# Earlier loads for batches 2 and 3, and x of batch 2 transposed entirely by DMA, in a one-core attention and MLP kernel

## Chip, cores, metric

One core of a Trainium2 chip. The metric is the device time of one execution in microseconds (us), the median over the executions named. Kernels are compared only within the same rounds.

## The reference, cut to what matters

```python
# q, k, v: (8 batches, 8 heads, 576 tokens, 64)
scores = q @ k.T / 8 + alibi_bias            # causal window of 128 tokens
x      = softmax(scores) @ v                 # -> (4608 tokens, 512)
h      = x @ w_in                            # 512 -> 2048   "first layer"
out    = (h * cos(h)) @ w_out                # 2048 -> 512   "second layer"
```

## The kernel before

The 4608 tokens are cut into nine chunks of 512. While chunk c goes through the layers, the attention of batch c + 1 is worked on in the gaps. The kernel has no fixed order of instructions: a list scheduler in the kernel's own Python (`Plan`) draws the order of every engine at build time from modelled durations. On the chip each engine follows that order and waits on semaphores where data is late.

A unit of attention (a head pair and 256 tokens, or the 64-token tail of a batch) ends with x in token-major form (`xnat`). The first layer needs it transposed (`xT`), in one of two ways: by a DMA that SyncE issues, or on TensorE into PSUM, from which ScalarE or VectorE copies it:

```python
def x_back(b, u, s, i):
    ...
    if b > 2 or (b == 2 and G):           # G: first (0) or second (1) 256 tokens of the batch
        o = op("sp", [lambda e: e.dma_start_transpose(xT[...], xnat[i][:, :])], ...)
        xops.append(o)
        return
    def f(e):                             # two 128x128 transposes on TensorE ...
        for r in range(2):
            ins = e.transpose(dst[:, 128*r:128*r+128], xnat[i][:, 128*r:128*r+128], ident[:, :])
        return ins
    op("pe", f, ...)
    flex(xT[:, pr, t0:t0 + 256], dst, ...)   # ... and a copy out of PSUM (ScalarE or VectorE)
```

The loads are issued by GpSimd, in program order, and cast from float32 to bf16. From the main loop:

```python
for c in range(NCH):
    ...                                   # first layer of chunk c
    if c + 1 < B:
        us = units(c + 1)
        if c == 0:
            play(1, SECOND)               # batch 1: its q and k are transposed on TensorE
        else:
            cross_transposes(c + 1)       # q, k of batch c + 1 by DMA
            if c == 1:
                load_v(2, after=crossed[3:4])   # waits for the fourth of these transposes
                load_qk(3)
                load_v(3)
            for g in range(0, 9, 3):
                run(us[g:g + 3], (1, 2, 3))
    if c == 0:
        load_qk(2)
    ...                                   # second layer of chunk c
R.schedule()
```

The softmax here doesn't subtract the row's maximum and nothing guards it: scores larger than these inputs give would overflow.

## Time and profile before

| | before |
|---|---|
| time, median of 3 | 313.05 us (312.87 to 313.22) |
| span of the profiled execution | 311.4 us |
| TensorE busy | 302.1 us, 97% |
| transposes of x on TensorE / by DMA (without tails) | 40 / 44 |
| GpSimd's wait ahead of V of batch 2 | 23.1 us |

To read the lines: a row of a timeline is start, duration, engine, line of the kernel, operation, output <- inputs, shapes, count, and in brackets the idle time before it with what ended it. A matmul's duration includes its way through the pipeline, so neighbours overlap; for the cost of one, take the distance from its start to the next start. In a list of waits a row is: who waited <- for whom: us in total, times, longest. The prediction below shows the page's main lines and reads them.

### The profile page before, as it was taken

What the parts mean: (1) busy time and instruction counts of PE and PEld (TensorE: products, weight loads), DVE (VectorE), ACT (ScalarE), POOL (GpSimd) and SP (SyncE); (2) the same over time, 40 slices, a digit from 0 to 9 for tenths busy, and PEclk for the clock granted to TensorE, in tenths of its full rate; (3) what the DMA queues carried; (4) which work ended last, traced back from release to release, by engine and by line L of the source; (5) the groups of instructions that cost most, each with busy time, mean ns of one, the idle gap of its engine ahead of it and who ended that gap; (6) DMA issues with size and microseconds to landing.
All of it is one profiled execution on the core that took longest, in us unless ns stands there. A gap on an engine that the chain in (4) does not pass through costs nothing.

```text
span 311.4 us, 6714 instructions
## 1 busy us (share of the span) xinstructions
PE 302.1 (97%) x2647; PEld 178.0 (57%) x2684; DVE 196.8 (63%) x444; ACT 206.7 (66%) x303; POOL 105.8 (34%) x134
## 2 busy tenths in 40 slices
PE   8799999999999999999999999999999999999996
PEld 4578546785578557845854554455445544444444
DVE  3798675786568757875887458766866882353000
ACT  7798936787588759773986488848873884462211
POOL 8999820069506300870537055505000000000000
DMA  9999999999939992999999999999823200101112
GB/s 131 166 193 193 192 171 193 164 105 167 189 76 121 154 171 47 120 152 191 141 175 158 176 138 108 147 169 138 144 59 103 70 8 2 68 0 67 69 67 101
DMA packets 159742, 38.97 MB, mean 125 GB/s; under 512 B 147808, under 2 KB 155232, under 8 KB 159712
## 3 DMA queue, kind: packets, MB, share of 16 engines
q0 software_dynamic: 109552, 18.10, 80.0%
q1 hardware_dynamic: 50160, 20.46, 33.5%
q8 instruction: 21, 0.34, 0.5%
q14 instruction: 9, 0.07, 0.1%
HBM read 36.70 MB, written 9.44 MB: 148 GB/s over the span
## 4 chain that ended last, share of the span: by engine, by line
PE 86%; DMA 8%; POOL 3%; issue 1%; DVE 1%; ACT 0%; POOLq 0%
PE ps L863 37%; PE ps L837 20%; PE ps L852 18%; DMA qnat<-in_q_dram 6%; PE ps L631 4%; PE ps L725 3%; DMA knat<-in_k_dram 2%; PE ps L728 2%; POOL vp L463 1%; PE ps L800 1%; PE ps L711 1%; PE ps L546 1%; PE ps L713 1%; PE ps L621 1%; POOL qnat L427 0%
## 5 line engine op out<-in xcount | busy, mean ns | idle before, releaser
L863 PE MATMUL ps<-w_outb,gT 128*128 128x512 bf16 (+2 forms) x564 | 133.7, 373 | 2.2 <-issue 0.8
L829 DVE TENSOR_TENSOR gT<-ps,cos 128x512 bf16<-128x512 f32 x144 | 94.8, 686 | 27.7 <-PE ps L863 14.0
L823 ACT ACTIVATE cos<-ps,halfpi 128x512 f32<-128x512 f32 x144 | 94.9, 687 | 20.9 <-PE ps L837 6.7
L863 PEld LDWEIGHTS ps<-w_outb,gT 128*128 128x128 bf16 x592 | 52.6, 98 | 53.1 <-issue 1.4
L668 ACT ACTIVATE p<-ps 128x768 bf16<-128x768 f32 (+1 forms) x64 | 54.8, 919 | 27.5 <-PE ps L631 15.3
L852 PE MATMUL ps<-xT,w_inb 128*128 128x256 bf16 x576 | 67.5, 273 | 0.0
L837 PE MATMUL ps<-xT,w_inb 128*128 128x512 bf16 x280 | 63.9, 379 | 0.6
L463 POOL DMA_DIRECT2D vp<-in_v_dram x40 | 34.8, 909 | 79.8 <-DMA xT<-xnat 35.2
L852 PEld LDWEIGHTS ps<-xT,w_inb 128*128 128x128 bf16 x576 | 54.5, 98 | 7.2 <-issue 0.5
L837 PEld LDWEIGHTS ps<-xT,w_inb 128*128 128x128 bf16 x288 | 27.3, 98 | 32.2 <-DVE xtail L756 1.1
L419 ACT ACTIVATE ob<-ps 128x512 f32<-128x512 f32 (+2 forms) x24 | 14.0, 582 | 44.2 <-PE ps L863 44.2
L454 POOL DMA_DIRECT2D qnat<-in_q_dram x32 | 29.3, 915 | 26.1 <-DMA xT<-xtail 26.1
L686 DVE TENSOR_TENSOR p<-p,emask 128x1024 bf16<-128x1024 bf16 x32 | 22.0, 688 | 13.7 <-ACT p L668 13.5
L454 POOL DMA_DIRECT2D knat<-in_k_dram x32 | 29.3, 917 | 2.1 <-PE ps L713 2.1
L767 DVE TENSOR_TENSOR xnat<-ps,rec 128x256 bf16<-128x256 f32 x64 | 26.8, 421 | 2.0
L725 PEld LDWEIGHTS ps<-vp,p 128*128 128x128 bf16 x256 | 17.0, 97 | 15.0 <-issue 8.8
L725 PE MATMUL ps<-vp,p 128*128 128x65 bf16 x256 | 21.9, 193 | 0.5 <-DVE p L686 0.4
L691 DVE TENSOR_TENSOR p<-p,emask 128x256 bf16<-128x256 bf16 x32 | 9.1, 283 | 17.6 <-ACT p L668 17.1
L728 PE MATMUL ps<-vp,p 128*128 128x65 bf16 x192 | 20.0, 193 | 0.0
L491 ACT ACT_TABLE_LOAD x15 | 19.2, 1283 | 0.3
L631 PEld LDWEIGHTS ps<-qt,kt 64*128 64x128 bf16 x320 | 12.0, 95 | 11.5 <-issue 7.8
L631 PE MATMUL ps<-qt,kt 64*128 64x128 bf16 (+1 forms) x320 | 18.4, 241 | 0.1
(58 smaller groups left out, 173.8 us busy)
## 6 DMA issues: line engine op xcount, KB each, us to landing
out_dram<-ob SPq DMA_DIRECT2D x35, 256.0 KB, 3.8
vp<-in_v_dram POOLq DMA_DIRECT2D x32, 128.0 KB, 5.9
knat<-in_k_dram POOLq DMA_DIRECT2D x25, 128.0 KB, 8.9
qnat<-in_q_dram POOLq DMA_DIRECT2D x25, 128.0 KB, 7.7
w_inb<-in_moe_w_in_dram POOLq DMA_DIRECT2D x8, 256.0 KB, 9.0
w_outb<-in_moe_w_out_dram POOLq DMA_DIRECT2D x6, 256.0 KB, 15.1
qnat<-in_q_dram POOLq DMA_DIRECT2D x3, 256.0 KB, 10.6
knat<-in_k_dram POOLq DMA_DIRECT2D x3, 256.0 KB, 13.3
```

The source lines that it names most:

```text
L454: op("pool", [lambda e: e.dma_start(nat[w][b % 2][0:rows, t, :].rearrange("p (h d) -> p h d", h=H), src[b, :, 128 * t:128 * t + rows, :].r ...
L463: op("pool", [lambda e, t=t, rows=rows: e.dma_start(vp[b % 2][0:rows, t, :, 0:64], v[b, :, 128 * t:128 * t + rows, :].rearrange("h p d -> ...
L631: ins = e.matmul(ps[:, banks[x], c0:c1], keys_ap(i, x, pr, kc), query_ap(i, x, pr, qb, nb), start=True, stop=True)
L668: op("act", lambda e: e.activation(P[i][:, :, lo:512], src_[:, :, lo:512], ACTF.Exp, scale=0.125), w=held + [("P", i)], occ=920 if u[1] el ...
L725: ins = e.matmul(o, P[i][:, x, d0:d0 + 128], V[:, kc, h, 0:65], start=True, stop=not two)
L728: ins = e.matmul(o, P[i][:, x, p0:p0 + 128], V[:, kc - 1, h, 0:65], start=False, stop=True)
L767: op("dve", lambda e: e.tensor_tensor(o, U[:, :, :, 0:64], rv[:, :, :, None].broadcast_to([128, 2, 2, 64]), ALU.mult), r=[("rec", ri)], w= ...
L823: op("act", lambda e: e.activation(cosb[ci][:, :], h, ACTF.Sin, bias=halfpi[:, 0:1]), r=["halfpi"], w=[("B", bank), ("cos", ci)], occ=586, ...
L829: op("dve", lambda e: e.tensor_tensor(o, h, cs, ALU.mult), r=[("cos", ci)], w=[("B", bank)] + keys, occ=606, lat=692, pri=3)
L837: op("pe", lambda e, kc=kc: e.matmul(ps[:, bank, :], w_in[:, kc, 128 * fc:128 * fc + 128], xT[:, kc, CH * c:CH * c + CH], start=(kc == 0), ...
L852: op("pe", lambda e, i=i, fc=fc, kc=kc: e.matmul(ps[:, bank, 256 * i:256 * i + 256], w_in[:, kc, 128 * fc:128 * fc + 128], xT[:, kc, t0:t0 ...
L863: op("pe", lambda e, fc=fc: e.matmul(ps[:, bank, 0:wd], gT[gi][:, fc, 128 * t:128 * t + 128], w_out[:, fc, c0:c0 + wd], start=(fc == 0), s ...
```

## The change

Its intent: GpSimd is freed from a 23 us wait, so that V of batch 2 and all of batch 3 come early, and TensorE is freed from the last eight transposes of x in batch 2. Moving the transposes' code into a helper, `cross`, and two new kinds of steps that no list uses, change nothing and are cut.

```diff
+XPE = [(b, u) for b in range(2) for u in range(8)]
...
-            if b > 2 or (b == 2 and G):
+            if (b, pr + 4 * G) not in XPE:
                 o = op("sp", [lambda e: e.dma_start_transpose(
...
                 else:
                     cross_transposes(c + 1)
-                    if c == 1:
-                        load_v(2, after=crossed[3:4])
-                        load_qk(3)
-                        load_v(3)
                     for g in range(0, 9, 3):
                         run(us[g:g + 3], (1, 2, 3))
             if c == 0:
                 load_qk(2)
+                load_v(2)
+                load_qk(3)
+                load_v(3)
```

More of the change, by code (lines that the diff above doesn't have):

```diff
@@ L580, in bass_alibi_sliding__then__act_gcu_kernel, with cross @@
         crossed = []
+        def cross(w, b, t0, behind=()):
+            i, t1 = b % 2, min(t0 + 2, NBLK)
+            rows = 128 if t0 < 4 else 64
+            return op("sp", [lambda e: e.dma_start_transpose(
+                tr[w][i][:, t0:t1, :, 0:rows].rearrange("p t k f -> p (t k) f"),
+                nat[w][i][0:rows, t0:t1, :].rearrange("p t f -> p (t f)"))],
+               r=[("nat", w, i, t) for t in range(t0, t1)],
+               w=[("tr", w, i, t, hf) for t in range(t0, t1) for hf in range(2)],
+               dma=f"x{w}{i}{t0}", occ=1250, pk=(1024 if t0 < 4 else 256, 0.92, True), pri=3,
+               behind=behind)
         def cross_transposes(b):
-            i = b % 2
             before = list(xops) if b > 2 else []
@@ L586, in cross_transposes @@
             crossed.clear()
-            for t0, t1 in ((0, 2), (2, 4), (4, 5)):
+            for t0 in (0, 2, 4):
                 for w in "qk":
-                    rows = 128 if t0 < 4 else 64
-                    o = op("sp", [lambda e, t0=t0, t1=t1, rows=rows, w=w: e.dma_start_transpose(
-                        tr[w][i][:, t0:t1, :, 0:rows].rearrange("p t k f -> p (t k) f"),
-                        nat[w][i][0:rows, t0:t1, :].rearrange("p t f -> p (t f)"))],
-                       r=[("nat", w, i, t) for t in range(t0, t1)],
-                       w=[("tr", w, i, t, hf) for t in range(t0, t1) for hf in range(2)],
-                       dma=f"x{w}{i}{t0}", occ=1250, pk=(1024 if t0 < 4 else 256, 0.92, True), pri=3,
-                       behind=before)
-                    crossed.append(o)
+                    crossed.append(cross(w, b, t0, before))
         def units(b):
@@ L892, in bass_alibi_sliding__then__act_gcu_kernel @@
         loads = {"k": lambda w, b, g: load_piece(w, {"q": q, "k": k}[w], b, g),
+                 "n": lambda w, b, t: load_nat(w, {"q": q, "k": k}[w], b, t),
                  "t": lambda w, b: load_nat(w, {"q": q, "k": k}[w], b, 4),
@@ L911, in play @@
                     first_tail(*a)
+                elif kind == "X":
+                    cross(a[0], b, a[1])
                 elif kind == "E":
```

## The prediction

> **What bounds the kernel now.** I read the page first (engine shares, then the chain that ended last), then the waits, then the timelines of the SyncE queue and of TensorE where batch 2 is worked on (70 to 103 us). The page:
>
> ```profile
> span 311.4 us, 6714 instructions
> PE 302.1 (97%) x2647; PEld 178.0 (57%) x2684; DVE 196.8 (63%) x444; ACT 206.7 (66%) x303; POOL 105.8 (34%) x134
> ...
> PE 86%; DMA 8%; POOL 3%; issue 1%; DVE 1%; ACT 0%; POOLq 0%
> ```
>
> TensorE is busy for 97% of the span and carries 86% of the chain. Matmuls overlap in the pipeline, so busy time alone proves little; I therefore took the distances between the starts of successive matmuls in the trace. They are 216 ns for 512 columns, 109 ns for 256, 29 ns for 65: evenly spaced streams. What TensorE loses beyond these distances from 70.6 us (the last first-layer matmul of chunk 1) to 102.5 us (that of chunk 2) sums to 0.9 us; in the next such stage, to 132.8 us, to 0.6 us. There is almost nothing to win by making anything arrive earlier. Only removing TensorE work shortens this kernel, unless a new wait appears.
>
> The change removes a large wait, so the list of waits matters next:
>
> ```profile
> POOL vp L463 <- DMA xT<-xnat: 35.2, 3, 13.5
> POOL qnat L454 <- DMA xT<-xtail: 26.1, 3, 14.0
> POOL vp L463 <- DMA kt<-knat: 23.1, 1, 23.1
> ```
>
> Columns: who waited for whom, us in total, times, longest. The third line is the wait that the change removes: GpSimd sat 23.1 us, from 41.95 to 65.05 us, until the fourth transpose of batch 2 had landed, before it issued the loads of V of batch 2, then q, k, v of batch 3. Impressive, but it is GpSimd's idle time, and no TensorE line of that list names a V load or a q/k transpose. Where batch 2's attention begins, TensorE's own timeline reads:
>
> ```profile
> 70.91 2.32 PE L863 MATMUL ps<-w_outb,gT 128*128 128x512 bf16 x10
> 73.16 0.67 PE L631 MATMUL ps<-qt,kt 64*128 64x256 bf16 x12
> ...
> 76.37 0.60 PE L863 MATMUL ps<-w_outb,gT 128*128 128x512 bf16 x2
> 76.80 0.28 PE L800 MATMUL ps<-ident,xnat 128*128 128x128 bf16 x2
> 76.92 0.38 PE L863 MATMUL ps<-w_outb,gT 128*128 128x512 bf16 x1
> ```
>
> The scores start at 73.16 us with no idle time in brackets, although kt had landed at 65.05 us: the q/k transposes have 8 us in hand. The L800 row is what the change does remove: two transposes of x through TensorE, squeezed between second-layer matmuls.
>
> **What the Trainium skill says.**
> - "TensorE: Matmul & The Clock Gate", section "Wait — 56ns, not 53.3ns?": warm 128-column matmuls start 55.6 ns apart. The trace agrees: median distance 56 ns after an L800 transpose.
> - "Perfetto Trace Analysis", section "Summary: the profiler window per engine type": the record of a GpSimd-issued DMA ends with descriptor generation and hides the movement. The trace agrees: the last q/k loads of batch 2 have records of some 0.7 us, yet landed 18 to 19 us after issue, near 60 us. So POOL's idleness from 42 us on isn't DMA idleness; the queue was still draining.
> - "DMA: Bandwidth & Descriptors", section "Queues, rings and completion order": each DMA engine takes turns between queues, packet by packet. The trace fits: q/k transposes issued from 60 to 65 us, with no load in flight, landed in 3.6 to 3.8 us; between 70 and 105 us, those of batch 3 beside loads took 7.7 to 8.0 us.
>
> **The change part by part.**
> 1. x of batch 2, first half. Four units (four head pairs, first 256 tokens) each lose two TensorE transposes and one PSUM-to-SBUF copy and gain one DMA transpose. From TensorE's timeline each pair of transposes delays the next matmul by 0.11 to 0.12 us (76.80 to 76.92; likewise at 77.81, 78.57 and 83.73). 8 x 56 ns = 0.45 us, all on the path, as TensorE's stream has second-layer work directly before and after each pair. The copies are 4 x 0.39 us = 1.6 us of ScalarE, at 66% busy: off the path. The four added DMA transposes cost SyncE's queue some 1.2 us of issue each, 5 us in all, in a stretch (72 to 84 us) where it has only three stores.
> 2. V of batch 2. It is issued right behind the q/k loads, near 42 to 46 us instead of 65.05 to 69.3. The same bytes. It is needed at 75.5 us (first P times V) and landed before at 70 to 74 us; no wait was there, so nothing is gained.
> 3. q, k, v of batch 3. The q/k buffers come free with batch 1's TensorE transposes (last at 48.23 us), the V buffer with batch 1's last P times V (58.94 us). Estimate from the issue durations of before (8.4 us for ten q/k loads, 4.3 us for five of V): q/k issued 48.5 to 57, V 59 to 63.5 us, instead of 69 to 82. The queue then drains without a pause. Before, the same twenty loads took from 65.05 us to about 86 us. Behind batch 2's q/k (until 60 us) and beside its transposes they should finish near 80 to 83 us: 3 to 6 us earlier, where no one needs them until 94 us.
> 4. Order. The program's order is planned at build time from modelled durations, so it will be redrawn from about 42 us on. A neighbouring stage tells what batch 2 may look like afterwards: batch 3 already takes all x by DMA. Between the last first-layer matmuls named above, batch 2's stage took 31.93 us and batch 3's 30.31. Of the 1.62, three more second-layer matmuls (56 against 53, counting missing records from gaps of 216 ns) are 0.65, the transposes 0.45, losses 0.91 less 0.59 are 0.32, and 0.2 stays unexplained. So a stage without TensorE transposes of x might save 0.45 to 0.8 us.
>
> Sum: 0.45 us surely removed, 0.1 us as a share of the possible 0.3: 313.05 - 0.55 = 312.5 us, or 0.2%.
>
> **The rivals.**
> - Loads against transposes. Batch 2's later q/k transposes now meet loads and land in some 8 us instead of 3.7. For it: the batch 3 figures. Against: they are issued by 66 us, the second score group needs them only at 79.64 us, the third at 85.50 us; 66 + 8 = 74. Even doubled, only the third group's tail is close. If it held, TensorE would stand at the scores for 1 to 4 us: 314 to 317 us.
> - x by DMA arrives too late for the next chunk. The first-layer matmuls of chunk 2 start at 87.59 us and need x of all four pairs. The fourth pair's x is normalised at 83.46 us; by DMA it lands after 3.3 us (what the one issued at 84.64 us, with loads about, took), at about 87. That is tight. Against a stall: batch 3 runs the same pattern, and TensorE's list has no wait for xT by DMA; second-layer matmuls can fill. If it held: 0.5 to 1.5 us lost, 313 to 314 us.
> - The removed 23.1 us wait sets the pace, and the kernel gains several us (306 to 309). For it: only its size. Against: TensorE lost 2 us in all from 60 to 130 us, which caps it.
> - The work goes and the new order gives as much back: 313.0 us.
>
> **Range and chances.** Most likely is a gain of 0.2 to 0.9 us. The runs of before spread over 0.35 us. Redrawing the order could add or take half a us. I take 311.6 to 313.4 us for 8 in 10. 2% would be 6.3 us either way: more than TensorE's losses allow on the one side, and on the other it needs a stall that the batch 3 stage doesn't show. Faster by over 2%: 0.01; within 2%: 0.98; slower by over 2%: 0.01.
>
> **What would show each step.** L800 transposes count 32 instead of 40, x transposes by DMA 48 instead of 44. The GpSimd wait of 23.1 us for kt is gone, and batch 3's loads are issued by about 64 us. TensorE's stage for batch 2 shortens by 0.4 to 0.8 us, and the later stages stay within 0.3 us. I am wrong if TensorE shows idle time before L631 or L852 named after a DMA at 73 to 95 us, if V of batch 2 becomes a wait, or if the span moves by over 1 us with TensorE's losses unchanged.

## The result

| | before | after |
|---|---|---|
| time, median of 4 | 312.96 us (312.56 to 313.22) | 312.96 us (312.77 to 313.81) |
| ratio after / before | | 1.0006 (95%: 0.9984 to 1.0029) |
| span of the profiled execution | 311.4 us | 311.0 us |
| transposes of x on TensorE / by DMA (without tails) | 40 / 44 | 32 / 48 |

A ratio is the mean time of one kernel's runs over that of the other's of the same rounds, so it is not quite the ratio of the medians. The time is the same. It lies inside the predicted range, but the predicted gain did not come, and the route is not the one I predicted. The page of the changed kernel (its line numbers are up to three higher: L855 is what was L852, L866 what was L863):

```profile
span 311.0 us, 6735 instructions
PE 302.8 (97%) x2676; PEld 177.0 (57%) x2676; DVE 196.2 (63%) x443; ACT 205.8 (66%) x300; POOL 105.7 (34%) x134
...
PE 91%; DMA 4%; DVE 2%; POOL 2%; issue 0%; ACT 0%; POOLq 0%
...
L855 PE MATMUL ps<-xT,w_inb 128*128 128x256 bf16 x576 | 67.6, 273 | 1.3 <-DMA xT<-xnat 1.3
```

The bound is as before. The last row is new: first-layer matmuls (group rows read "busy, mean ns | idle before, released by") stood 1.3 us for a DMA transpose of x. Before, that line's idle time was 0.0, and the first of chunk 2's first-layer matmuls ran without a pause:

```profile
L852 PE MATMUL ps<-xT,w_inb 128*128 128x256 bf16 x576 | 67.5, 273 | 0.0
87.59 0.82 PE L852 MATMUL ps<-xT,w_inb 128*128 128x256 bf16 x6
```

GpSimd's waits in the changed kernel:

```profile
POOL qnat L455 <- DMA xT<-xtail: 40.8, 3, 29.5
POOL vp L464 <- DMA xT<-xnat: 36.0, 3, 12.9
POOL vp L464 <- DMA xT<-xtail: 21.1, 1, 21.1
POOL vp L464 <- issue: 4.7, 6, 1.4
```

The wait of 23.1 us for kt is gone. The idle time went to a later wait, which grew from 14.0 to 29.5 us, and to pauses of 0.2 to 1.4 us between the new loads ("issue": nothing the profile shows was waited for). TensorE's timeline where chunk 2's first layer begins (rows of P times V between them left out), and there the row that the prediction had named as what would prove it wrong:

```profile
84.29 1.47 PE L866 MATMUL ps<-w_outb,gT 128*128 128x512 bf16 x6
85.59 0.49 PE L855 MATMUL ps<-xT,w_inb 128*128 128x256 bf16 x3
87.38 0.50 PE L855 MATMUL ps<-xT,w_inb 128*128 128x256 bf16 x3 [1.29 <-DMA xT<-xnat]
```

The first three first-layer matmuls take head pairs 0, 1 and 2; the fourth needs pair 3 and stands. By start distances the loss is 1.46 us. Pair 3's transpose was issued at 81.56 us. The DMA issues of the changed kernel (output <- input, queue, operation, count, us from issue to landing), first those of 81 to 82 us, then the V load among those of 65 to 67 us, the last of batch 3:

```profile
xT<-xnat SPq DMA_TRANSPOSE x1, 5.8
```

```profile
vp<-in_v_dram POOLq DMA_DIRECT2D x1, 64.0 KB, 21.7
```

So x of pair 3 landed at 87.33 us, directly behind the last load, which was issued at 65.34 and landed at 87.00 us. Before, the last of these loads landed at 86.91 us: in this pair of traces, issuing them 16 us earlier did not bring their end forward. Over all traces below it did by some 2 us (88.8 us on average in the four with late loads, 87.0 in the eight with early ones).

**Why not.** The DMA engines were already busy. Before, from 40 to 60 us the loads in the queue had a share of 156%, and from 70 to 86 us 199% (packets of several loads overlap, hence over 100). The early loads joined that queue, and batch 2's q/k transposes, which had had the engines to themselves from 60 to 65 us (3.2 to 4.3 us each to land), now shared them (7.6 to 10.8 us). This is read from the shares and the landings; no run tested it by itself.

**What the plan thought.** The kernel's own build-time model can be printed. This is no measurement; it is what the order was drawn from:

```
changed kernel               planned    measured
last V load of batch 3 lands   80.87       87.00
x of pair 3 issued             81.70       81.56
x of pair 3 lands              84.65       87.33
first-layer matmuls start      85.64       85.59
```

The model has everything right but the end of the load queue, by 6 us. With x expected at 84.65 us it put first-layer matmuls at 85.64, while eleven second-layer matmuls of chunk 1 that waited for nothing were left for later.

### The profile page after: what moved, and what is told of

The parts are those of the page before. It is cut to its first block, busy times and chain, and to the rows that moved or that the text cites. A ratio compares the mean times of both kernels' runs of the same rounds, so it can differ in the third digit from the quotient of the medians.

```text
span 311.0 us, 6735 instructions
## 1 busy us (share of the span) xinstructions
PE 302.8 (97%) x2676; PEld 177.0 (57%) x2676; DVE 196.2 (63%) x443; ACT 205.8 (66%) x300; POOL 105.7 (34%) x134
## 4 chain that ended last, share of the span: by engine, by line
PE 91%; DMA 4%; DVE 2%; POOL 2%; issue 0%; ACT 0%; POOLq 0%
PE ps L866 39%; PE ps L855 20%; PE ps L840 20%; PE ps L634 4%; PE ps L728 3%; DMA knat<-in_k_dram 2%; DMA xT<-xnat 2%; PE ps L731 2%; PE ps L547 1%; PE ps L714 1%; PE ps L716 1%; DVE p L689 1%; PE ps L624 1%; POOL vp L464 1%; PE ps L803 1%; DVE emtail L528 0%
## 5 line engine op out<-in xcount | busy, mean ns | idle before, releaser
L866 PE MATMUL ps<-w_outb,gT 128*128 128x512 bf16 (+2 forms) x592 | 137.9, 374 | 0.0
L866 PEld LDWEIGHTS ps<-w_outb,gT 128*128 128x128 bf16 x592 | 52.7, 98 | 53.3 <-issue 1.6
L855 PE MATMUL ps<-xT,w_inb 128*128 128x256 bf16 x576 | 67.6, 273 | 1.3 <-DMA xT<-xnat 1.3
L840 PE MATMUL ps<-xT,w_inb 128*128 128x512 bf16 x288 | 64.8, 379 | 0.0
L855 PEld LDWEIGHTS ps<-xT,w_inb 128*128 128x128 bf16 x576 | 54.5, 98 | 8.7 <-DMA xT<-xnat 1.6
```

Source lines behind the costliest of these rows:

```text
L840: op("pe", lambda e, kc=kc: e.matmul(ps[:, bank, :], w_in[:, kc, 128 * fc:128 * fc + 128], xT[:, kc, CH * c:CH * c + CH], start=(kc == 0), ...
L855: op("pe", lambda e, i=i, fc=fc, kc=kc: e.matmul(ps[:, bank, 256 * i:256 * i + 256], w_in[:, kc, 128 * fc:128 * fc + 128], xT[:, kc, t0:t0 ...
L866: op("pe", lambda e, fc=fc: e.matmul(ps[:, bank, 0:wd], gT[gi][:, fc, 128 * t:128 * t + 128], w_out[:, fc, c0:c0 + wd], start=(fc == 0), s ...
```

## The experiments

Theory A: taking x off TensorE saves time, and a wait for x of pair 3 gives it back; the wait exists because loads are in the queue until 87 us and because the plan did not know it. Theory B: the end of the DMA queue sets the pace whatever the order. Theory C: all this is scatter. Theory D came with the results: a redrawn order gains by luck elsewhere.

**A measure inside the trace.** Times scatter by 1 us and more, and the traces show where: the first 71 us, where TensorE waits here and there for the first loads, whatever the variant. From the start of the last cosine of chunk 1 (69.5 to 72.8 us) to the end of TensorE's last matmul, the "rest", things are steady. TensorE's weight loads, of which no record is missing, show that the comparison is fair: their sequence is the same in all fourteen traces up to 75 us (the prediction had expected a new order from 42 us on), and the rest holds the same work in every version, 528 second-layer and 608 first-layer matmuls among it, but for the transposes of x (8, 2 or 0). Here are all traces. "Loss" is the time lost by start distances at the first-layer matmuls that wait for x; the landing times come from the trace's semaphore events.

| kernel | last V load of batch 3 lands | x of pair 3 lands | loss, us | rest, us | rest less loss |
|---|---|---|---|---|---|
| before | 86.91 | (TensorE) | 0 | 237.99 | 237.99 |
| before, again | 89.37 | (TensorE) | 0 | 237.97 | 237.97 |
| early loads only | 85.29 | (TensorE) | 0 | 237.97 | 237.97 |
| after | 87.00 | 87.33 | 1.46 | 238.62 | 237.16 |
| after, again | 86.96 | 87.32 | 0.93 | 238.11 | 237.18 |
| after, third | 87.53 | 87.75 | 1.76 | 238.90 | 237.14 |
| V of batch 3 late | 94.83 | 83.66 | 1.63 (at 95 us) | 238.89 | 237.26 |
| plan told 1.35 us | 87.60 | 88.05 | 0.88 | 237.91 | 237.03 |
| plan told 2.7 us | 87.38 | 87.81 | 0 | 237.25 | 237.25 |
| plan told 2.7 us, again | 88.18 | 88.57 | 0.71 | 237.87 | 237.16 |
| x by DMA only | 88.85 | 91.00 | 0.27 | 237.41 | 237.14 |
| x by DMA only, again | 90.12 | 90.19 | 0.34 + 1.13 | 238.55 | 237.08 |
| pair 3 on TensorE | 85.86 | (TensorE) | 0 | 237.27 | 237.27 |
| V of batch 3 left out | none | 84.86 | 0 | 237.21 | 237.21 |

The last column holds the answer. Without the eight transposes TensorE's rest is 237.03 to 237.26 us, plus whatever it waits for x (237.27 with two of the eight, "pair 3 on TensorE"). With them it is 237.97 to 237.99 us. The difference is 0.8 us, and the wait costs what it lasts.

Not all of the 0.8 us is the transposes. The three traces with the old order on TensorE (before, before again, early loads only) also lose 0.29 us near 270 us, where first-layer matmuls start only after VectorE's product `gT`; none of the eleven others has this wait. In the chain of the kernel before (start, us, what):

```profile
263.08 6.49 PE ps L863 x30
269.58 0.70 DVE gT L829
270.33 5.35 PE ps L837 x24
```

The redrawn orders happen not to have it; nobody planned that. The other 0.5 us falls in the stage of chunk 2 (from the last cosine of chunk 1 to that of chunk 2): 31.93 us before, with 58 second-layer matmuls in it, against 30.94 with 56 (V of batch 3 left out) and 31.61 with 59 (plan told 2.7 us). At 0.216 us for each of those, that is 0.53 to 0.56 us.

### The control: the changed kernel again

No edit.

> The changed kernel unchanged, as a control. Theory A (a wait): TensorE again stands 1.2 to 1.6 us before a first-layer matmul of chunk 2 near 87 us, for x of batch 2's fourth head pair by DMA, which lands within 0.5 us of the last load of V of batch 3 (near 87 us); time 312.6 to 313.4 us, ratio to before 0.998 to 1.001. Theory C (only noise): the wait is gone or of another size, as it came from one execution.

Measured: 312.93 us, before 312.51 (ratio 1.0006, 0.9984 to 1.0028). The wait is there again, with a loss of 0.93 us, a little under the range given:

```profile
87.36 0.50 PE L855 MATMUL ps<-xT,w_inb 128*128 128x256 bf16 x3 [0.77 <-DMA xT<-xnat]
```

Chunk 1 had ended 0.5 us later here (70.47 us against 69.95), and the wait was 0.5 us shorter; it ended at the same time, 87.36 us. TensorE's lead turned into waiting. Theory C falls.

### The plan is told that x lands 2.7 us later

```diff
 class Op:    # + slot "late"
-            d.end = t + (self.DONE if de != "pool" else ...)
+            d.end = t + d.late + (self.DONE if de != "pool" else ...)
 ...
-                   pk=(256, 0.92, True), pri=2)
+                   pk=(256, 0.92, True), pri=2, late=2700 if b == 2 and not G else 0)
```

> The same loads, transposes and data; only the model that draws the program's order at build time is told that the four x transposes of batch 2's first half land 2.7 us later than it thought, so that TensorE does second-layer matmuls of chunk 1 (some ten were left) in the place of the wait. Theory A: the loss near 87 us falls from 1.46 us to under 0.4 us and the time by 0.8 to 1.4 us against the control, to about 311.7 us (ratio to before 0.995 to 0.998). Theory B (the DMA queue's end sets the pace, whatever the order): the wait moves or stays, the time stays within 0.3 us of the control. Theory C: no change beyond 0.3 us.

Measured: 311.72 us against 312.93 for the control on the same chip; ratio to before 0.9969 (0.9949 to 0.9988). x of pair 3 landed at 87.81 us, no earlier, but TensorE had other work:

```profile
86.46 0.27 PE L856 MATMUL ps<-xT,w_inb 128*128 128x256 bf16 x1
86.56 0.81 PE L867 MATMUL ps<-w_outb,gT 128*128 128x512 bf16 x3
87.46 0.71 PE L856 MATMUL ps<-xT,w_inb 128*128 128x256 bf16 x5
```

(Line numbers are one higher in this kernel.) One first-layer matmul, three second-layer ones (a unit's P times V stands between the last two rows), then first-layer ones of pairs 0 to 2, and none of them waits. The gain is 1.2 us, inside the expected 0.8 to 1.4. Theory B falls in its strong form: with the queue ending when it ended, another order is faster.

### V of batch 3 held back

```diff
                 load_qk(3)
-                load_v(3)
             else:
+                if c == 1:
+                    load_v(3, after=xops[3:4])
```

> Loads of V of batch 2 and of q and k of batch 3 stay early; the five loads of V of batch 3 are held until x of batch 2's fourth pair has landed. Theory A and B both: the load queue runs dry near 80 to 82 us instead of 87, x of the fourth pair lands in 3 to 4.5 us after issue instead of 5.8, at about 85.5 us, and TensorE's wait falls below 0.4 us; time 311.5 to 312.1 us (ratio 0.995 to 0.998). If the wait stays with the queue empty, both are wrong about the cause.

Measured: 313.17 us, ratio 1.0014 (0.9991 to 1.0037): a miss. The first half came as expected: x of pair 3 landed at 83.66 us, 2.5 us after issue, and nothing stood at 87 us. But the held loads now ran from 84 us, into the x transposes of the second 256 tokens; those issued at 87 to 88 us took 6.8 to 7.8 us. Built again, its plan has TensorE's order of the changed kernel up to 94 us and brings nine first-layer matmuls forward there; that was not enough, and TensorE met the late transposes at 95 us:

```profile
92.77 0.82 PE L855 MATMUL ps<-xT,w_inb 128*128 128x256 bf16 x6
95.06 1.16 PE L855 MATMUL ps<-xT,w_inb 128*128 128x256 bf16 x9 [1.47 <-DMA xT<-xnat]
```

The wait moved by 8 us and kept its size. My expectation forgot what the held loads would collide with.

### V of batch 3 left out

So the loads have to be taken away, not moved. The result is wrong in batch 3; the order on TensorE, VectorE, ScalarE and SyncE is exactly that of the changed kernel (the two plans, built again, agree).

```diff
                 load_qk(3)
-                load_v(3)
```

> The changed kernel without its five loads of V of batch 3 (so batch 3 gives a wrong result, on purpose): the suspected cost is taken away, not moved, and the order of instructions on TensorE, VectorE, ScalarE and SyncE is the same as in the changed kernel. Theory A and B: the load queue runs dry near 80 us, x of batch 2's fourth pair lands near 84 us, TensorE's wait near 87 us (0.9 and 1.5 us in the two executions of the changed kernel) falls below 0.2 us, and chunk 2's stage takes about 31.0 us for its 31.8 to 32.3; no wait appears at 95 us either. Time about 312.0 us, ratio 0.995 to 0.999. If the wait stays, the loads of V of batch 3 are not what delays x.

Measured: 311.56 us, before 313.02 (ratio 0.9964, 0.9949 to 0.9979). Between 81 and 82.5 us its DMA issues read:

```profile
xT<-xnat SPq DMA_TRANSPOSE x1, 3.4
```

x of pair 3 landed at 84.86 us, and TensorE went through:

```profile
84.21 1.47 PE L866 MATMUL ps<-w_outb,gT 128*128 128x512 bf16 x6
85.52 0.82 PE L855 MATMUL ps<-xT,w_inb 128*128 128x256 bf16 x6
86.42 0.82 PE L855 MATMUL ps<-xT,w_inb 128*128 128x256 bf16 x6
```

Chunk 2's stage took 30.94 us for the changed kernel's 32.33 and 31.80. With the order the same, the loads in the queue are shown to be what delays x. The time fell a little further than I expected (312.0).

### Pair 3 on TensorE again

```diff
-XPE = [(b, u) for b in range(2) for u in range(8)]
+XPE = [(b, u) for b in range(2) for u in range(8)] + [(2, 3)]
```

> As the changed kernel, but x of the fourth pair of batch 2's first half goes through TensorE again; little else in the order differs. Theory A: the wait near 87 us shrinks to what the third pair's x by DMA leaves (it landed at 85.2 to 85.6 us, the first-layer matmuls start at 85.7 us), under 0.3 us; the two transposes cost 0.11 us; chunk 2's stage about 31.1 to 31.3 us; time 311.7 to 312.3 us. Theory B: the wait stays as long, on another pair.

Measured: 311.96 us, ratio 0.9969 (0.9955 to 0.9984), no wait for x, stage of chunk 2 31.00 us. As expected. TensorE's order is the changed kernel's with this one pair of transposes put in. The pair costs 0.06 us against the version with V left out (rest 237.27 against 237.21 us), where 0.11 had been expected.

### The early loads alone

```diff
+XPE = ... + [(2, u) for u in range(4)]      # x of batch 2's first half on TensorE, as before
```

> The early loads alone; x of batch 2's first half goes through TensorE as before. My step on the loads says they are worth nothing: no wait for x at 87 us, 40 TensorE transposes of x, last load of V of batch 3 landing near 87 us as in both kernels; time within 0.3 us of before (ratio 0.999 to 1.001), and 0.45 us or more above the versions that have no TensorE transposes and no wait. A rival: the early loads save some 0.5 to 1 us by themselves (the changed kernel was 1.0 us ahead at the start of batch 2), then 312.0 to 312.5 us.

Measured: 313.01 us, ratio 1.0010 (0.9989 to 1.0032); rest 237.97 us against 237.99 before. TensorE's order is that of the kernel before throughout, so this is a clean test: the early loads by themselves are worth nothing, within 0.02 us. The rival in the expectation, that they gave the changed kernel its lead of 1.0 us at 70 us, falls: in the traces that lead comes and goes with the kernel unchanged (69.95, 70.47 and 70.07 us after; 70.97 and 70.64 before).

### x by DMA alone, loads as before

```diff
+                    if c == 1:
+                        load_v(2, after=crossed[3:4])
+                        load_qk(3)
+                        load_v(3)
...
                 load_qk(2)
-                load_v(2)
-                load_qk(3)
-                load_v(3)
```

> x of batch 2's first half by DMA alone, with the loads where they were before (behind batch 2's fourth q/k transpose). The last load of V of batch 3 lands at 86.5 to 88 us as before, so x of the fourth pair lands at 87 to 88 us, as late as in the changed kernel; but here the build-time model sees the loads late and plans x for 87.6 us, putting six second-layer matmuls ahead. Theory A: no wait over 0.4 us near 87 us, stage of chunk 2, corrected for second-layer matmuls left over, 0.4 to 0.6 us shorter than before, time 312.0 to 312.5 us. Theory B: a wait of 1 us or more as in the changed kernel. Were the early loads worth something, this would be slower than the kernel with the early loads and the corrected plan (311.7 us) by more than 0.5 us.

Measured: 313.60 us, ratio 1.0022 (1.0006 to 1.0038), an interval above 1: a miss. In its trace (of the slowest of the six executions) the loss at x is small, 0.27 us, and the rest, 237.41 us, is 0.58 us better than before, as expected. But the first 34 us took 36.84 us: TensorE stood 1.6 us for a load of batch 0, and the granted clock of that stretch was 0.90.

> A repeat of x by DMA with the late loads, whose time missed the expectation (313.6 us for 312.0 to 312.5) although from the end of chunk 1's first layer on it was 0.58 us faster than the kernel before (237.41 us). In that execution the first 34 us, whose TensorE order is the changed kernel's, took 2.5 us longer, after a 1.6 us wait for a k load of batch 0 and a granted clock of 0.90 there. If that was chance: 34.0 to 35.0 us this time and 312.2 to 312.7 us. If the kernel itself brings it: again 35.5 us or more and a time over the kernel before; 237.3 to 237.6 us for the rest in either case.

Measured: 313.32 us, ratio 1.0004 (0.9979 to 1.0030): a miss again, otherwise than the first time. The first chunk ended at 34.08 us, so the slow start was that execution's and not the kernel's. But the rest took 238.55 us, with this wait:

```profile
90.23 0.28 PE L855 MATMUL ps<-xT,w_inb 128*128 128x256 bf16 x1 [0.97 <-DMA xT<-xnat]
```

Here the last V load landed only at 90.12 us and x of pair 3 at 90.19; the plan had counted on 87.64. So with x by DMA the early loads do matter. The first expectation had named the test, over 0.5 us slower than the version with early loads and the corrected plan, and it is met: 313.32 against 312.33 us. Issued late, the loads ended at 88.9 and 90.1 us in the two traces (86.9 and 89.4 in those of the kernel before), issued early between 85.3 and 88.2 us in eight. What the two parts do together is not the sum of what each does alone. How much of this kernel's time (312.5 to 314.5 us in twelve executions) is such a wait and how much the scatter of the first 34 us stays open: only two of the twelve have a trace, and each shows one of the two.

### The plan told half as much

Edit as above, with 1350 in place of 2700.

> The build-time model told half as much (1.35 us later instead of 2.7). Its plan puts one second-layer matmul more ahead of the first first-layer matmul that needs the fourth pair, for which it then plans 86.19 us, against a landing near 87.4 us. Theory A: the wait near 87 us stays, at 0.5 to 1.3 us, and the time lies between the control and the version told 2.7 us: 312.2 to 312.9 us. Theory D (the gain of the version told 2.7 us came from its redrawn order elsewhere, not from the wait): no relation, the time may be anything from 311.5 to 313, with the stages away from chunk 2 differing.

Measured: 312.59 us, ratio 0.9990 (0.9977 to 1.0002), the loss 0.88 us. Between control and full dose, as theory A says, though the interval just includes 1; the rest less the loss, 237.03 us, is that of the others.

### Repeats on a third chip

> The kernel before unchanged, for a second trace. From the end of chunk 1's first layer to TensorE's last matmul it took 237.99 us, and the version with the early loads alone 237.98. If that measure is as steady as it looks, 237.9 to 238.1 us here, with no wait over 0.4 us after 71 us; what scatters is the time up to there, by up to 1 us, as between the other executions.

Measured: rest 237.97 us, as expected. That the measure is steady is what lets single traces be compared above. Time 313.10 us, ratio 1.0000.

> A repeat, on another chip, of the version whose plan was told 2.7 us. Theory A: 237.2 to 237.4 us from the end of chunk 1's first layer to the last matmul (237.25 before), no wait near 87 us, and a time 0.25 to 0.45% under the kernel before. Theory D (luck): the gain isn't repeated.

Measured: 312.33 us, ratio 0.9971 (0.9945 to 0.9997), as expected; but the trace has a wait of 0.71 us, against the expectation, because in this execution the last V load landed at 88.18 us and x at 88.57, 0.8 us later than in the first trace. Less that, its rest is 237.16 us. 2.7 us is not quite enough a margin. Against theory D: the rest less the loss is the same in versions whose order differs from 86 us on (told 2.7 us) and in those that keep the changed kernel's (V left out, pair 3 on TensorE). So luck in the order does not explain the gain over the changed kernel. Over the kernel before it explains some 0.3 us, the wait at 270 us.

> The changed kernel a third time, beside the repeats. Theory A: the wait ends when x of the fourth pair lands, at 87.2 to 87.5 us, wherever chunk 1's first layer ended; so if that end is at T, the wait is about 87.35 less (T + 15.9) us, and the time from T to the last matmul is 237.2 us plus the wait. Time within 0.2% of the kernel before.

Measured: 313.16 us, ratio 1.0000 (0.9972 to 1.0028). The loss was 1.76 us where the formula gives 1.38: the wait ended at 87.80 us, outside my 87.2 to 87.5, as the last V load landed at 87.53 and x at 87.75 us. The wait follows the load queue, not the clock on the wall. The rest, 238.90 us, is 237.14 plus the loss; I had said 237.2.

**The better version.** The plan told 2.7 us beats the kernel before by 0.3% on two chips (ratios 0.9969 and 0.9971, both intervals under 1), and the changed kernel by 1.2 and 0.8 us in the medians. Of the 0.8 us that its rest, less the loss, is shorter than before, some 0.3 us is the wait at 270 us that its order happens not to have. Pair 3 on TensorE does as well (0.9969), without touching the model.

## Why the prediction was right or wrong

The time was right: 312.96 us for 312.5, inside 311.6 to 313.4, and within 2% as said. But the gain of 0.2 to 0.9 us that it called most likely did not come (ratio 1.0006). By its steps:

1. *x of batch 2's first half, 0.45 to 0.8 us saved on TensorE.* Right: 0.53 to 0.56 us in the stage of chunk 2, of which it spoke, where the sum used 0.55. One step towards it was miscounted: batch 2's stage has five second-layer matmuls more than batch 3's, not three (58 against 53 by the weight loads; matmul records are missing), so 1.08 us, and with the 0.45 of the transposes only 0.09 of the 1.62 us is left. The rest as a whole shortened by 0.8 us; the remaining 0.25 us or so lies in later stages, where the wait of 0.29 us at 270 us is gone, which the prediction did not foresee.
2. *V of batch 2 early gains nothing.* Right, for all the early loads together: 237.97 against 237.99 us.
3. *The queue then drains near 80 to 83 us.* Wrong: 87.0 us, and 85.3 to 88.2 in the other traces with early loads. The estimate took the twenty loads' 21 us of before, started them at 60 us and allowed 2 us at most for the transposes beside them. Of the pause that it meant to fill, batch 2's transposes already used 60 to 65 us; now they ran beside the loads. That they took the missing time is likely but not tested.
4. *The rival "x by DMA arrives too late for the next chunk", 0.5 to 1.5 us, 313 to 314 us.* This is what happened: 0.93 to 1.76 us in three traces. The step that failed is its dismissal. "By DMA it lands after 3.3 us" followed from one transpose at the end of the load queue (issued at 84.64 us, the last load landing at 86.91); it took 5.2 to 6.1 us. "Batch 3 runs the same pattern" overlooked that hardly a load is left in the queue there at the time that counts: batch 3's fourth x transpose was issued at 113.8 us (113.2 in the changed kernel) and landed 2.3 us later, the last load landing at 114.0 us (113.2). "Second-layer matmuls can fill" is true, but only if the order drawn at build time puts them there, and it was drawn for x at 84.65 us.
5. *The rival "loads against transposes".* The landings of 7.6 to 10.8 us are as it feared; the score groups at 77.6 and 83.5 us did not wait. Rightly put aside. The prediction's 3.6 to 3.8 and 7.7 to 8.0 us are medians: single q/k transposes took 3.2 to 4.3 us from 60 to 65 us, the later two landing beside the first V loads, and batch 3's took 3.2 to 9.3 us.
6. *The removed wait of 23.1 us.* Rightly taken for worthless, and the reason given (TensorE loses too little) held.

So a gain of 0.8 us and a wait of 0.9 to 1.8 us cancelled in these traces. That the time still fell near the forecast is luck, not the mechanism that was forecast.

## What to carry to other kernels

When a transfer moves work off the bounding engine, ask what is in the DMA queues at the moment it is issued: here an x transpose of batch 2 landed in 2.3 to 4.4 us when issued after the last load had landed, and in 5.2 to 8.7 us when loads already queued went on landing for some 5 us or more. Issuing loads earlier need not end them much earlier when the DMA engines are already busy: here 16 us earlier at the start gave about 2 us at the end. An order that is fixed at build time hides a late transfer only if the model knows that it is late, so compare its planned landings with the trace's before changing anything else.

## What the Trainium skill lacked or had wrong

- "DMA: Bandwidth & Descriptors", section "Anatomy of one DMA — SWDGE (gpsimd) path", gives about 2.0 us plus bytes over bandwidth for one DMA. It lacks what a load costs behind others: here a V load landed 3.6 us after issue with no other load queued (65.05 us, before), and those of batch 3 21 to 24 us after issue in the changed kernel's queue.
- The same page, section "Queues, rings and completion order", describes the turns between queues, which no run here tests packet by packet, and has no figure for what they cost: an x transpose of batch 2 took 2.3 to 4.4 us when issued after the last load had landed and 5.2 to 8.7 us when loads already queued went on landing for some 5 us or more.
- No page says whether GpSimd can issue loads without limit ahead of their landing. With loads landing over 20 us after issue it paused for 0.2 to 1.4 us between V loads, 4.7 us in six pauses, where the kernel before had none. Whether a full ring or something else does this was not tested.
- "TensorE: Matmul & The Clock Gate", section "Part 4: PE-mode transpose", gives the duration of a 128x128 transpose (about 275 ns in a kernel). What counts in a stream is the start distance, 56 ns here (duration 219 ns); that section does not give it for transposes.
